# One core, attention with one shared key head beside a Mish MLP: a new order of the products of the first stage

## The chip, the cores and the metric

The kernel runs on one core of one Trainium2 chip. The metric is the device time of one execution in microseconds; three executions of the kernel before took 1537.57 to 1537.7 us, the median is 1537.6.

## What is computed

```python
x = A_x                                    # [1, 2048, 512]
xn = layernorm(x)                          # over the last axis, eps 1e-5, no weights
q = (xn @ wq)                              # 32 heads of 16
k, v = xn @ wk, xn @ wv                    # one head of 16 for all
p = softmax(q k^T / 4)                     # 2048 x 2048 for each head
attention = concat(p v) @ wo               # 512 -> 512
h = xn @ w1 + b1                           # 512 -> 1792
mlp = (h * tanh(softplus(h))) @ w2         # Mish, 1792 -> 512
out = x + attention + mlp
```

All is fp32 outside. Inside, a product of two fp32 tensors is made of three passes over rounded parts: each tensor is stored as an upper part (the value rounded to the narrower format of the TensorE pass) and a lower part (what the rounding left), and the terms upper·upper, upper·lower and lower·upper are summed in one PSUM bank (`TERMS`).

## The kernel before

**Two stages.** The first stage (lines 829 to 1044) loads and normalises the tokens, transposes them, multiplies them by the query and key/value weights, starts two tiles of the MLP, and takes the 32 first pairs of scores, from which the row maxima for the first head group come. The second stage goes through a written plan (`PLAN`, one token per piece of work) with all other scores, exponentials, products with V and MLP tiles. It stays as it was; its first TensorE instruction is a pair of scores at L555.

**Tokens and tiles.** The 2048 tokens are four chunks of 512, called 0 to 3. A chunk has four query tiles of 128 rows (q*c*_*mt*) and one key/value tile (kv*c*). A tile of product is 12 matmuls of 128 x 512 (four slices of the depth, three terms) into one PSUM bank. The key/value tiles of chunks 0 and 1, the first query tile and the two first MLP tiles `hidden(0)` and `hidden(1)` are multiplied in this way, in full height, one after another (L796).

**Products by halves.** From then on, two tiles (a word of two letters: piece k and l are the key/value tiles of chunks 2 and 3, the other letters the next query tiles in order) are multiplied side by side: one step is two matmuls of 64 of the 128 rows (L781), one in each half of the array, one for each tile, each into its own bank. A word has 24 steps: 12 in the first order, then 12 with the halves of the two tiles exchanged. Since the exchanged half adds to a bank that the other half of the array wrote, TensorE drains (L957) before the second order, unless two pairs of scores since then show that the first order is done. `HALVES` lists phases: a word stands for six steps, a digit for half of the transposes of that chunk, the star for one query tile in full height, into bank 7. The pairs of banks for the words are (4, 5) and (6, 7), given out in turn (`places`).

**Pairs of scores.** A pair (`first_pair`, L555) is two matmuls side by side, of 128 queries by 512 keys each, and one reduction on DVE (L572) over both banks; two pairs of banks alternate. The 32 pairs go by key chunk: pairs 0 to 7 read keys 0, pairs 8 to 15 keys 1, and so on; pair 24 is the first to read keys 3. Between two pairs the recorder takes steps by a credit of `PACE` (11, from pair 20 on 9; a step of two matmuls costs 2), so a pair falls into a phase wherever the credit ends.

**What hangs on a product.** When a key/value tile is done, ACT copies it out of its bank (L475) and rounds it into KS (L477), and POOL writes the lower part of the keys, in two steps (L433, `KS<-kvs,KS`). When a query tile is done, ACT copies it out (L507) and rounds it (L513), POOL writes its lower part (L433, `q<-q`), and SP stores it. A transposed chunk gets its lower part on POOL too (L433, `X<-pt,X`). The MLP tiles 0 and 1 go through Mish, a chain of ACT steps (L738 to L753), one short DVE step (L742) and five products (L747, L759 to L763) on POOL; the last four of them are on DVE if all first scores are done when they are recorded.

**What sets the order.** All of this is recorded by one program in the order in which it stands on each engine. Lower parts and Mish are not recorded at once but put off (`later`) by so many pairs, and recorded when due or when their reader is (`flush`); each engine's queue keeps that order and does not pass a waiting instruction.

Of the kernel before, what the change touches and what calls it, by code (L numbers as in the profile page):

```python
# [20 lines left out]
NT = CT // P  # L21
DT = D // P
FT = F // P
KT = S // P
KC = S // CT
# [8 lines left out]
U_MAX = 16384.0  # L34
WARM = 44
QBUFS = 6
PACE = 11, 9
HALVES = "qr 2 qr 2 qr qr tk tk uv tk tk uv 3 uv 3 uv wl wl wl wl xy xy ab ab ab ab xy xy cd cd ef ef cd cd ef ef *"

TERMS = ((0, 0), (0, 1), (1, 0))  # L40

# [139 lines left out]
def attention_and_mlp(ctx: ExitStack, tc: tile.TileContext, x, wq, wk, wv, wo, w1, b1, w2, out):  # L181
    nc = tc.nc
    E = mybir.EngineType
    PE, SP = nc.tensor, nc.sync
# [16 lines left out]
    def bank(tag, name, bufs):  # L201
        return BANK[{"o": 6, "misc": 7}[tag]]

    def misc(name):
        return bank("misc", name, 1)
# [11 lines left out]
    def product_bank():  # L217
        return BANK[given.pop(0)]
# [8 lines left out]
    def later(delay, stage, tag, step=None):  # L227

        queue.append((now[0] + delay if step is None else step, stage, tag))
# [218 lines left out]
    def project(w, c, hi_first=False):  # L448
        order = [(d, i, j) for d in range(DT) for i, j in TERMS]
        if hi_first:  # L450
            order.sort(key=lambda term: term[2])
        return [(w(i, d), X[c][:, j, d]) for d, i, j in order]

    def keys_values(c, every=3):
# [41 lines left out]
    def queries(c, mt):  # L496
        if mt not in WQ:
            WQ[mt] = query_block(mt)
        wb = WQ[mt].rearrange("p a (t f) -> p a t f", t=DT)
        yield 3 * DT, (("wq", mt),)  # L500
        flush(("wq", mt))
        turn[0] += 1
        p = product_bank() if halving[0] else bank("o", f"q{c}_{mt}", 1) if turn[0] % 2 else misc(f"q{c}_{mt}")
        yield p, project(lambda i, d: wb[:, i, d], c, c == mt == 0)
        q = first.tile([P, 2, CT], F32R, tag="q", name=f"q{c}_{mt}", bufs=QBUFS)
        qf = q.bitcast(F32)
        ACT.activation(qf[:, 1], p, AF.Copy)  # L507
        yield
        last = c * DT + mt >= NC * DT - 3
        if last:  # L510
            POOL.tensor_copy(q[:, 0], qf[:, 1])
        else:
            ACT.activation(q[:, 0], qf[:, 1], AF.Copy)  # L513

        def rest():
            below(DVE if scored[0] and not last else POOL, q[:, 1], qf[:, 1], q[:, 0])
            d = scratch.tile([2, P, CT], F32, tag="q", name=f"q{c}_{mt}_dram", bufs=NC * DT)
            for g in range(2):
                u = c * UPC + 2 * mt + g
                if u:  # L520
                    if g == 0 or u == 1:
                        SP.dma_start(out=d.rearrange("k p n -> p k n"), in_=qf)
                    LOADS[u] = lambda u=u, g=g: load(u, g)
                    if u < QTS:
                        later(0, LOADS[u], ("q", u))
                    continue
                QS[u] = QT[u % QTS]
                for a in range(2):
                    r = (2 * g + a) * 2 * DH
                    for k, part in enumerate((0, 1, 0)):  # L530
                        to = a * 64 + k * DH
                        SP.dma_start(out=QS[u][to : to + DH].bitcast(F32), in_=qf[r : r + 2 * DH, part])

            def load(u, g):
                QS[u] = QT[u % QTS]
                for a in range(2):
                    r = (2 * g + a) * 2 * DH
                    for to, n in ((0, 2), (2 * DH, 1)):
                        SP.dma_start(
                            out=QS[u][a * 64 + to : a * 64 + to + n * DH].bitcast(F32),  # L540
                            in_=d[:n, r : r + 2 * DH].rearrange("k (d pair) n -> k d (pair n)", pair=2),
                        )

        later(1, rest, ("q", c, mt))
        yield
# [180 lines left out]
    def hidden(f):  # L726

        yield 3 * DT, (("w1", f),)
        flush(("w1", f))
        p = misc(f"h0_{f}") if f else bank("o", f"h0_{f}", 1)  # L730
        wb = WB[f].rearrange("p a (t f) -> p a t f", t=DT)
        yield p, project(lambda i, d: wb[:, i, d], 0)
        h, n = TH[f], TN[f]
        u, z, r = (first.tile([P, CT], F32, tag=t, name=f"{t}{f}", bufs=1) for t in ("fu", "fz", "fr"))
        ACT.activation(h, p, AF.Identity, bias=b1s[:, f : f + 1])

        def exponential():
            ACT.activation(u, h, AF.Exp)  # L738
            later(1, square, ("u", f))

        def square():
            DVE.tensor_scalar_min(u, u, U_MAX)  # L742
            later(1, product, ("u", f))

        def product():
            ACT.activation(n, u, AF.Copy, bias=2.0)
            POOL.tensor_tensor(out=n, in0=n, in1=u, op=ALU.mult)  # L747
            later(2, quotient, ("u", f))

        def quotient():  # L750
            ACT.activation(z, n, AF.Ln, bias=2.0)
            ACT.activation(r, z, AF.Exp, scale=-1.0)
            mish(h, n, z, r, lambda out, x: ACT.activation(out, x, AF.Copy, scale=-2.0, bias=2.0), DVE if scored[0] else POOL)  # L753

        later(max(1, 8 + 4 * f - 100 - now[0]), exponential, ("u", f))

    def mish(h, n, z, r, affine, engine=POOL):

# [69 lines left out]
    with tc.tile_pool(name="first", bufs=1) as first:  # L828
# [55 lines left out]

        flush(("wq", 0))
        first_transposes()
        split_block()
        first_keys = keys_values(0, 1)
        for _ in range(4):
# [9 lines left out]
        run(first_keys)  # L899
        while first_queries.product():  # L900
            pass
        turned = banks[:, 1, :FT]
        PE.transpose(turned, b1_rows, ident[:FT, :FT])
        ACT.activation(b1s, turned, AF.Copy)
        flush(("q", 0, 0))
        root(1, DVE)
# [21 lines left out]
        def phases():  # L928
            opened, turning = {}, {}
            for word in HALVES.split():  # L930
                if word.isdigit():
                    if word not in turning:
                        turning[word] = transposes_by_halves(int(word))
                    for cost in turning[word]:
                        if not cost:
                            break
                        yield cost
                    continue
                if word == "*":
                    piece = ready.pop(0)  # L940
                    given[:] = [7]
                    while piece.product():
                        done[0] += 1
                        yield 2
                    done[0] += 1
                    continue
                if word not in opened:
                    b = places.pop(0)
                    given[:] = b, b + 1
                    both = [Piece(keys_values_by_halves(2 + (k == "l"))) if k in "kl" else ready.pop(0) for k in word]  # L950
                    for piece in both:
                        piece.begin()
                    opened[word] = b, both, [(order, k) for order in range(2) for k in range(3 * DT)]
                b, both, todo = opened[word]
                for order, k in todo[: 3 * DT // 2]:
                    if order and not k and known[0] < both[-1]:
                        PE.drain()  # L957
                        known[0] = emitted[0]
                    last = [both[lane ^ order].half(k, lane, order) for lane in range(2)]
                    if last[1]:  # L960
                        both[1].end()
                        both[0].end()
                    emitted[0] += 1
                    done[0] += 1
                    if k + 1 == 3 * DT:
                        both.append(emitted[0])
                    yield 2
                del todo[: 3 * DT // 2]
                if not todo:
                    places.append(b)  # L970
                    del opened[word]
                    if not (opened or scores_left[0] or ready):
                        return
# [10 lines left out]
            while n > 0 and ready:  # L984
                n -= fill_slot(n)

        scores_left, credit, steps = [len(range(KC * NT * 2))], 0, phases()
        order = [(kc, qt, pair) for kc in range(KC - 1) for qt in range(NT) for pair in range(2)]
        order += [(KC - 1, qt, pair) for pair in range(2) for qt in range(NT)]
        for i, (kc, qt, pair) in enumerate(order):  # L990
# [4 lines left out]
            if i == 7:  # L995
                root(3, POOL)
                normalise(3, POOL)
            credit += PACE[i >= 20] + (6 if i in (1, 2) else 0)
            while credit > 0:
                credit -= next(steps, credit)  # L1000
            if i == 1:
                rooted(3)
            run_due(2)
            if i == 22:
                for a in range(2):
                    r = slice(a * 64 + 48, a * 64 + 50)
                    SP.dma_start(out=KS[r].bitcast(F32), in_=ones[:, None].to_broadcast([2, KT, P]))
            if i in (7, 9, 15):
                flush(("v", (7, 9, 15).index(i)))
            if 8 <= i < 16 or 20 <= i < 24:  # L1010
                c = (1, 2, 3, 3)[(i - 8) // 4]
                flush(("lo", c))
# [261 lines left out]
```

## Time and profile before

| | |
|---|---|
| median of three executions | 1537.6 us |
| profiled execution, its own time | 1537.76 us |
| its span | 1536.0 us |
| instructions on TensorE, busy | 11767, 1528.4 us |
| first pair of scores starts | 28.95 us |
| first TensorE instruction of the planned stage | 90.84 us |
| mean granted TensorE clock | 1.000 |

In the timeline rows a line starts with the time from the start of the span and the duration, then the engine, the line of the kernel, the operation, the tile written and the tiles read, their shapes and the number of instructions that are put together in the row; a bracket gives how long the engine had stood idle and who released it. PE is TensorE, DVE VectorE, ACT ScalarE, POOL GpSimd. Two matmuls that go side by side in the two halves of the array start within some nanoseconds of each other, and each has a record of its own. In a table of windows, "x" counts matmuls that lie in the window.

### The profile page before, as it was taken

To read this page: it belongs to the slowest core of one execution; us is meant where nothing else is said; L and a number is where in the kernel's file an instruction comes from. 1 tells how busy PE (TensorE), PEld (TensorE's weight loads), DVE (VectorE), ACT (ScalarE), POOL (GpSimd) and SP (SyncE) were. 2 spreads that over 40 slices of the span, in tenths; PEclk is the share of its full clock that TensorE was granted. 3 is DMA by queue.
4 is the path that set the end of the run, shared out by engine and by line. 5 is a ranking of instruction groups with operands and counts; after the bars stand their busy time and mean duration, and the time that the engine had idled before them with its cause. 6 is when DMAs were issued, how large, how long until landed. Compare 5 with 4: busy or idle time off the path is not lost.

```text
span 1536.0 us, 30659 instructions
## 1 busy us (share of the span) xinstructions
PE 1528.4 (100%) x11767; PEld 852.0 (55%) x11767; DVE 1353.4 (88%) x2166; ACT 1298.2 (85%) x2301; POOL 887.4 (58%) x838
## 2 busy tenths in 40 slices
PE   9999999999999999999999999999999999999998
PEld 7865555555555555545555555555555545555555
DVE  7899899898998898999989999989988998999842
ACT  6478888988989888887888888888888888888896
POOL 6769675776656546644655575454255844554641
PEclk9999999999999999999999999999999999999999
DMA  5755122243122231142413231033222133032220
GB/s 188 291 195 191 42 81 87 101 151 113 38 65 80 94 101 40 54 135 95 123 41 127 94 108 51 31 115 117 71 88 91 56 92 94 32 101 95 70 92 34
DMA packets 65479, 148.37 MB, mean 97 GB/s; under 512 B 10886, under 2 KB 20180, under 8 KB 64948
## 3 DMA queue, kind: packets, MB, share of 16 engines
q1 hardware_dynamic: 65332, 146.41, 29.2%
q8 instruction: 93, 1.52, 0.4%
q14 instruction: 54, 0.44, 0.1%
HBM read 98.51 MB, written 47.45 MB: 95 GB/s over the span
## 4 chain that ended last, share of the span: by engine, by line
PE 98%; POOL 1%; DVE 0%; ACT 0%; DMA 0%; issue 0%; SPq 0%; POOLq 0%
PE banks L637 33%; PE banks L1084 24%; PE banks L633 19%; PE banks L555 18%; PE banks L781 3%; PE banks L796 1%; PE banks L718 1%; PE banks L458 0%; POOL X L433 0%; DMA pt<-in_A_x_dram 0%; DVE ysb L708 0%; PE banks L397 0%; PE banks L419 0%; POOL KS L433 0%; POOL wq L433 0%
## 5 line engine op out<-in xcount | busy, mean ns | idle before, releaser
L567 DVE TENSOR_REDUCE nm<-banks 128x1 f32<-128x512 f32 x1770 | 1117.2, 684 | 107.5 <-PE banks L555 62.2
L1160 ACT ACTIVATE pt<-banks 128x512 f32<-128x512 f32 x1618 | 871.4, 603 | 130.8 <-PE banks L633 70.6
L555 PE MATMUL banks<-KS,QS 48*128 48x512 f32 x2048 | 688.0, 420 | 0.0
L633 PE MATMUL banks<-QS,KS 64*128 64x512 f32 x2048 | 686.9, 417 | 0.0
L637 PE MATMUL banks<-pt,V 128*32 128x512 f32 x4096 | 534.5, 603 | 0.0
L633 PEld LDWEIGHTS banks<-QS,KS 64*128 64x128 f32 x2048 | 333.1, 184 | 220.4 <-DVE nm L567 81.1
L555 PEld LDWEIGHTS banks<-KS,QS 48*128 48x128 f32 x2048 | 329.4, 184 | 196.5 <-DVE nm L567 94.1
L1084 PE MATMUL banks<-ring,act 64*128 64x512 f32 x1344 | 333.4, 397 | 0.2
L1084 PE MATMUL banks<-X,wblk 64*128 64x512 f32 x1296 | 330.2, 395 | 0.3
L1152 ACT ACTIVATE pt<-banks 128x1024 f32<-128x1024 f32 x215 | 219.5, 1025 | 47.7 <-PE banks L633 27.6
L1084 PEld LDWEIGHTS banks<-X,wblk 64*128 64x128 f32 x1296 | 214.0, 185 | 27.9 <-issue 10.7
L1084 PEld LDWEIGHTS banks<-ring,act 64*128 64x128 f32 x1344 | 213.1, 185 | 28.7 <-issue 12.0
L637 PEld LDWEIGHTS banks<-pt,V 128*32 128x32 f32 x4096 | 86.5, 108 | 181.7 <-issue 172.1
L759 POOL TENSOR_TENSOR tn<-tn,tr 128x512 f32<-128x512 f32 x54 | 69.4, 1285 | 192.8 <-ACT tr L1170 192.8
L1165 POOL TENSOR_SCALAR tu<-tu 128x512 f32<-128x512 f32 x54 | 80.3, 1487 | 157.5 <-ACT tu L1164 157.5
L581 DVE TENSOR_REDUCE nm<-banks 128x2 f32<-128x1024 f32 x107 | 130.1, 1219 | 10.6 <-PE banks L555 6.5
L1098 POOL TENSOR_TENSOR ysb<-ysb,ty 128x512 f32<-128x512 f32 x64 | 82.1, 1286 | 86.9 <-ACT ty L1097 86.9
L251 POOL TENSOR_TENSOR act<-th,act 128x512 fp32r<-128x512 f32 x56 | 72.1, 1287 | 32.8 <-ACT act L250 24.0
L761 POOL TENSOR_TENSOR tz<-tz,tn 128x512 f32<-128x512 f32 x54 | 69.5, 1288 | 4.5
L1167 POOL TENSOR_TENSOR tn<-tn,tu 128x512 f32<-128x512 f32 x54 | 69.5, 1288 | 4.5
L763 POOL TENSOR_TENSOR th<-th,tz 128x512 f32<-128x512 f32 x54 | 69.6, 1288 | 4.2
L762 POOL TENSOR_TENSOR th<-th,tn 128x512 f32<-128x512 f32 x55 | 70.9, 1289 | 0.0
(140 smaller groups left out, 1042.0 us busy)
## 6 DMA issues: line engine op xcount, KB each, us to landing
wblk<-w_dram SPq DMA_DIRECT2D x42, 512.0 KB
ring<-w_dram SPq DMA_DIRECT2D x42, 512.0 KB
q_dram<-q SPq DMA_DIRECT2D x16, 512.0 KB
QS<-q_dram SPq DMA_DIRECT2D x62, 128.0 KB
o_dram<-ov SPq DMA_DIRECT2D x31, 256.0 KB
raw_w<-in_B_w_dram SPq DMA_DIRECT2D x28, 256.0 KB
w_dram<-wblk SPq DMA_DIRECT2D x14, 512.0 KB
w_dram<-ring SPq DMA_DIRECT2D x14, 512.0 KB
```

The source lines that it names most:

```text
L251: POOL.tensor_tensor(out=lo, in0=src, in1=hi.bitcast(F32), op=ALU.subtract)
L555: PE.matmul(tile, QS[u][rows, pair, qt * P : (qt + 1) * P], KS[rows, kc * CT : (kc + 1) * CT], start=True, stop=True,)
L567: DVE.tensor_reduce(out=m[:, a : a + 1], in_=tile, axis=AX.X, op=ALU.max)
L581: DVE.tensor_reduce(out=m, in_=tiles, axis=AX.X, op=ALU.max)
L633: PE.matmul(bank, KS[rows, kt * P : (kt + 1) * P], QS[u][rows, pair], start=True, stop=True)
L637: PE.matmul(BANK[7][h * 32 : (h + 1) * 32], V[:, kt], PT.pop((u * KT + kt) * HG + h), start=kt == 0, stop=kt == KT - 1,)
L762: engine.tensor_tensor(out=h, in0=h, in1=n, op=ALU.mult)
L1084: PE.matmul(self.p, w[rows], x[rows], start=self.first, stop=not any(self.todo))
L1098: POOL.tensor_tensor(out=YS[t], in0=YS[t], in1=ty, op=ALU.add)
L1152: ACT.activation(slots[slot // 2], banks[:, bank : bank + 2], AF.Exp, scale=SCALE)
L1160: ACT.activation(PT[n], BANK[bank], AF.Exp, scale=SCALE)
L1165: POOL.tensor_scalar_min(tu, tu, U_MAX)
```

## The change

`HALVES` is written anew, as phases with a point wherever a pair of scores is to stand; `PACE` and its credit go. Up to the two words wl and xy a phase has six steps as before, with a pair between phases; from the second half of wl on, a phase has four steps (`:4`), so three pairs stand between the three phases of half a product. Seven words are multiplied by halves instead of eight, and the last three query tiles (`*6 *4 *7`, the digit is the bank) in full height instead of one. The first query tile goes to bank 7's pool (`misc`) where it went to bank 6, the transpose of b1 is put ahead of the first products, the terms of the first products stand in another order (`hi_first`), Mish of the MLP tiles starts two pairs' time sooner, and the V steps are recorded at pairs 7, 12 and 17.

```diff
-PACE = 11, 9
-HALVES = "qr 2 qr 2 qr qr tk tk uv tk tk uv 3 uv 3 uv wl wl wl wl xy xy ab ab ab ab xy xy cd cd ef ef cd cd ef ef *"
+HALVES = (
+    ". qr . qr 2 . qr 2 . qr . tk . tk . uv . uv . tk . tk . uv . 3 . uv . 3 "
+    ". xy . xy . wl . wl . xy . xy . wl:4 . wl:4 . wl:4 . ab:4 . ab:4 . ab:4 . cd:4 . cd:4 . cd:4 . ab:4 . ab:4 . ab:4 "
+    "cd cd *6 *4 *7"
+)
...
-            order.sort(key=lambda term: term[2])
+            order.sort(key=lambda term: (term[2], term[1]))
...
-        p = product_bank() if halving[0] else bank("o", f"q{c}_{mt}", 1) if turn[0] % 2 else misc(f"q{c}_{mt}")
+        p = product_bank() if halving[0] else misc(f"q{c}_{mt}")
...
-        later(max(1, 8 + 4 * f - 100 - now[0]), exponential, ("u", f))
+        later(max(1, 6 + 4 * f - 100 - now[0]), exponential, ("u", f))
...
+        turned = banks[:, 1, :FT]
+        PE.transpose(turned, b1_rows, ident[:FT, :FT])
         split_block()
...
-        turned = banks[:, 1, :FT]
-        PE.transpose(turned, b1_rows, ident[:FT, :FT])
...
             for word in HALVES.split():
+                word, _, n = word.partition(":")
+                n = int(n or 3 * DT // 2)
...
-                if word == "*":
+                if word == ".":
+                    yield 0
+                    continue
+                if word[0] == "*":
                     piece = ready.pop(0)
-                    given[:] = [7]
+                    given[:] = [int(word[1])]
...
-                for order, k in todo[: 3 * DT // 2]:
+                for order, k in todo[:n]:
...
-            credit += PACE[i >= 20] + (6 if i in (1, 2) else 0)
-            while credit > 0:
-                credit -= next(steps, credit)
+            while scores_left[0] and next(steps):
+                pass
...
-            if i in (7, 9, 15):
-                flush(("v", (7, 9, 15).index(i)))
+            if i in (7, 12, 17):
+                flush(("v", (7, 12, 17).index(i)))
```

Three places show how the instructions move (line numbers of the kernel after are 3 larger up to about L766 and 8 larger at the end).

POOL, around the lower parts of the keys of chunk 3 (`KS<-kvs_871` before), before the change; tn, fz and th with 76, 360 and 73 belong to Mish of MLP tile 0:

```order
L433 TENSOR_TENSOR q_1_786<-q_1_786 128x512
L433 TENSOR_TENSOR q_0_789<-q_0_789 128x512
L433 TENSOR_TENSOR KS<-kvs_871,KS 16x512 x2
L433 TENSOR_TENSOR q_2_874<-q_2_874 128x512
L747 TENSOR_TENSOR tn_76<-tn_76,fu_359 128x512
L759 TENSOR_TENSOR tn_76<-tn_76,fr_361 128x512
L761 TENSOR_TENSOR fz_360<-fz_360,tn_76 128x512
L762 TENSOR_TENSOR th_73<-th_73,tn_76 128x512
L763 TENSOR_TENSOR th_73<-th_73,fz_360 128x512
```

The same place after the change (`KS<-kvs_952`):

```order
L436 TENSOR_TENSOR q_1_749<-q_1_749 128x512
L436 TENSOR_TENSOR q_0_752<-q_0_752 128x512
L750 TENSOR_TENSOR tn_76<-tn_76,fu_359 128x512
L436 TENSOR_TENSOR q_3_894<-q_3_894 128x512
L436 TENSOR_TENSOR q_2_897<-q_2_897 128x512
L762 TENSOR_TENSOR tn_76<-tn_76,fr_361 128x512
L764 TENSOR_TENSOR fz_360<-fz_360,tn_76 128x512
L765 TENSOR_TENSOR th_73<-th_73,tn_76 128x512
L766 TENSOR_TENSOR th_73<-th_73,fz_360 128x512
L436 TENSOR_TENSOR KS<-kvs_952,KS 16x512 x2
L436 TENSOR_TENSOR q_0_955<-q_0_955 128x512
```

Before, the two key steps stood ahead of Mish and behind the lower parts of two queries; now they stand behind the four last steps of Mish, behind the lower parts of the two queries of xy (q_3_894, q_2_897).

TensorE, around pair 24, the first that reads keys 3, with what each waits for, before; the products are those of the word ab (wq_120, wq_122):

```order
L781 MATMUL banks<-X_470,wq_120 128x512
L781 MATMUL banks<-X_470,wq_122 128x512
L781 MATMUL banks<-X_470,wq_120 128x512
L781 MATMUL banks<-X_470,wq_122 128x512
L555 MATMUL banks<-KS,QS_88 128x512 [waits DVE_49,Pool_49]
L555 MATMUL banks<-KS,QS_88 128x512 [waits Pool_49]
L781 MATMUL banks<-X_470,wq_120 128x512
L781 MATMUL banks<-X_470,wq_122 128x512
```

After, from pair 23 on; the last step of wl stands directly ahead of these rows:

```order
L558 MATMUL banks<-KS,QS_88 128x512 [waits DVE_49]
L558 MATMUL banks<-KS,QS_88 128x512
L784 MATMUL banks<-X_482,wq_120 128x512 [waits Activation_49]
L784 MATMUL banks<-X_482,wq_122 128x512
L784 MATMUL banks<-X_482,wq_120 128x512
L784 MATMUL banks<-X_482,wq_122 128x512
L784 MATMUL banks<-X_482,wq_120 128x512
L784 MATMUL banks<-X_482,wq_122 128x512
L784 MATMUL banks<-X_482,wq_120 128x512
L784 MATMUL banks<-X_482,wq_122 128x512
L558 MATMUL banks<-KS,QS_88 128x512 [waits DVE_49,Pool_49]
L558 MATMUL banks<-KS,QS_88 128x512 [waits Pool_49]
```

The pair waits for POOL in both. In the new order the last step of wl stands one pair and one phase of four steps ahead of it; in the old one wl's last step (`X_705,wkv` with `X_363,wq_122`, at the place below) stands four whole pairs with the phases of xy and ab between them ahead:

```order
L555 MATMUL banks<-KS,QS_88 128x512 [waits DVE_49]
L555 MATMUL banks<-KS,QS_88 128x512
L781 MATMUL banks<-X_705,wkv 128x512
L781 MATMUL banks<-X_363,wq_122 128x512
L781 MATMUL banks<-X_363,wq_128 128x512 [waits Activation_49]
L781 MATMUL banks<-X_470,wq_103 128x512
```

TensorE at the end of the first stage, before; wq_128 in full height is the star, and the L555 below it the planned stage's first:

```order
L781 MATMUL banks<-X_705,wq_122 128x512
L781 MATMUL banks<-X_705,wq_120 128x512
L796 MATMUL banks<-X_705,wq_128 128x512 [waits Activation_49]
L796 MATMUL banks<-X_705,wq_128 128x512 x11
L555 MATMUL banks<-KS,QS_89 128x512 [waits DMAHW3_49,DMAHW2_49,Activation_49]
L633 MATMUL banks<-QS_88,KS 128x512 [waits DMAHW5_49,DMAHW3_49,DVE_49]
```

After:

```order
L784 MATMUL banks<-X_714,wq_103 128x512
L784 MATMUL banks<-X_482,wq_128 128x512
L799 MATMUL banks<-X_714,wq_120 128x512 [waits Activation_49]
L799 MATMUL banks<-X_714,wq_120 128x512 x11
L799 MATMUL banks<-X_714,wq_122 128x512 x12
L799 MATMUL banks<-X_714,wq_128 128x512 x12
L558 MATMUL banks<-KS,QS_89 128x512 [waits DMAHW3_49,DMAHW2_49,Activation_49]
L636 MATMUL banks<-QS_88,KS 128x512 [waits DMAHW4_49,DMAHW3_49,DVE_49]
```

One tile in full height has become three; both times the first of them waits for ACT, and the others wait for nothing.

More of the change, by code (lines that the diff above doesn't have):

```diff
@@ L967, in phases @@
                     yield 2
-                del todo[: 3 * DT // 2]
+                del todo[:n]
                 if not todo:
@@ L985, in fill_slots @@
                 n -= fill_slot(n)
-        scores_left, credit, steps = [len(range(KC * NT * 2))], 0, phases()
+        scores_left, steps = [KC * NT * 2], phases()
+        next(steps)
         order = [(kc, qt, pair) for kc in range(KC - 1) for qt in range(NT) for pair in range(2)]
```

## The prediction, made before the changed kernel was run

> **What bounds the kernel now.** First the page: busy shares, and the chain of work that ended last.
>
> ```profile
> PE 1528.4 (100%) x11767; PEld 852.0 (55%) x11767; DVE 1353.4 (88%) x2166; ACT 1298.2 (85%) x2301; POOL 887.4 (58%) x838
> ...
> PE 98%; POOL 1%; DVE 0%; ACT 0%; DMA 0%; issue 0%; SPq 0%; POOLq 0%
> ```
>
> TensorE works all the time and is itself the chain: a microsecond in which it stands anywhere is a microsecond on the end. So I read the timeline of PE over the first stage, where all edits lie, up to its last query tile and the first pair of scores of the planned stage.
>
> ```profile
> 28.95 0.50 PE L555 MATMUL banks<-KS,QS 48*128 48x512 f32 x2
> ...
> 64.20 0.41 PE L555 MATMUL banks<-KS,QS 48*128 48x512 f32 x2
> ...
> 65.36 0.41 PE L555 MATMUL banks<-KS,QS 48*128 48x512 f32 x2
> ...
> 67.92 0.41 PE L555 MATMUL banks<-KS,QS 48*128 48x512 f32 x2
> ...
> 69.67 0.40 PE L555 MATMUL banks<-KS,QS 48*128 48x512 f32 x2
> ...
> 87.85 3.06 PE L796 MATMUL banks<-X,wq 128*128 128x512 f32 x12
> 90.84 0.50 PE L555 MATMUL banks<-KS,QS 48*128 48x512 f32 x1
> ```
>
> Pairs of scores start at 28.95; the planned stage starts at 90.84 and its instructions are the same after the change, so the change is worth what it moves 90.84. From 64.20 to 65.36 stand one pair and four steps: five slots in 1.16 us, **0.233 us a slot** (a slot is one pair or one step, each two matmuls side by side). Between 28.95 and 90.84 both kernels have the same 236 slots. So the change can only move waits, drains and the clock.
>
> **The change part by part.** *The start.* The eviction of the first query tile holds the bank into which the first MLP tile is multiplied.
>
> ```profile
> 16.57 1.08 PE L796 MATMUL banks<-X,wq 128*128 128x512 f32 x4
> 17.58 0.23 PE L903 MATMUL banks<-ident,b_rows 14*128 14x14 f32 x1
> 18.57 3.02 PE L796 MATMUL banks<-X,wblk 128*128 128x512 f32 x12 [0.76 <-ACT q L507]
> ```
>
> With the query in the other bank and the b1 transpose earlier, the 0.76 goes, and with it about 0.1 of restart and 0.1 in the new order of the first terms: **−1.0** (−0.7 to −1.2).
>
> *Drains.* Six slots from 67.92 to 69.67 should take 6 × 0.233 = 1.40 and took 1.75: the drain ahead of the second order of a product costs 0.35. The old program has six of these at L957 and the new one has one: 5 × 0.35 = **−1.75**.
>
> *Old waits.* A pause between two steps ends at 57.46:
>
> ```profile
> 57.02 0.39 PE L781 MATMUL banks<-X,wq 64*128 64x512 f32 x1
> 57.46 0.49 PE L781 MATMUL banks<-X,wkv 64*128 64x512 f32 x1
> ```
>
> 0.44 instead of a slot's 0.233, and a like one for the tokens before it: **−0.3**.
>
> *New small waits.* The products come sooner after their tokens. The lower parts of chunk 2 end on POOL at 34.95 + 4.92 = 39.87; TensorE asks for them at about 39.6, by slots counted from the new first pair at 27.9 (an estimate):
>
> ```profile
> 34.95 4.92 POOL L433 TENSOR_TENSOR X<-pt,X 128x1024 fp32r<-128x1024 f32 x2
> ```
>
> I put 0.4 there, 0.35 where xy takes the banks that uv has just left, 0.15 for chunk 3: **+0.9** (0 to 1.3; nothing below, as a wait gives no time).
>
> *The keys of chunk 3* (the piece called l, in wl). Pair 24 is the first to read them, and waits for POOL's two lower-part steps. Before, wl was multiplied out at 61.64, eight microseconds ahead of pair 24 at 69.67:
>
> ```profile
> 61.64 0.39 PE L781 MATMUL banks<-X,wkv 64*128 64x512 f32 x1
> ...
> 62.12 0.60 ACT L475 ACTIVATE kvs<-banks 128x512 f32<-128x512 f32 x1 [4.70 <-issue]
> ...
> 63.09 0.63 ACT L477 ACTIVATE KS<-kvs 128x512 fp32r<-128x512 f32 x1
> ...
> 63.86 2.66 POOL L433 TENSOR_TENSOR KS<-kvs,KS 16x512 fp32r<-16x512 f32 x2 [3.97 <-ACT KS L477]
> ```
>
> Done at 66.52, they were 3.15 us early. Now wl ends one pair and four steps ahead of pair 24: from its last half, 6 slots = 1.4 us, while the rows above need 66.52 − 61.64 = 4.9. That alone is a wait of 3.5. POOL's order makes it longer: two lower parts of xy's queries and four steps of Mish now stand ahead of the two key steps, which stood ahead of Mish before. The durations:
>
> ```profile
> 72.44 1.09 ACT L507 ACTIVATE q<-banks 128x512 f32<-128x512 f32 x2 [0.79 <-PE banks L781]
> 73.42 1.16 ACT L513 ACTIVATE q<-q 128x512 fp32r<-128x512 f32 x2
> ```
>
> ```profile
> 71.13 1.29 POOL L759 TENSOR_TENSOR tn<-tn,fr 128x512 f32<-128x512 f32 x1 [2.00 <-ACT fr L752]
> 72.50 1.50 POOL L761 TENSOR_TENSOR fz<-fz,tn 128x512 f32<-128x512 f32 x1
> 73.95 1.29 POOL L762 TENSOR_TENSOR th<-th,tn 128x512 f32<-128x512 f32 x1
> 75.32 1.30 POOL L763 TENSOR_TENSOR th<-th,fz 128x512 f32<-128x512 f32 x1
> 76.58 2.54 POOL L433 TENSOR_TENSOR q<-q 128x512 fp32r<-128x512 f32 x2
> ```
>
> From the start of xy's last half: 0.41 for it, 1.61 until the first query is rounded (72.44 to about 74.05), 0.1 over to POOL, 2.54 for two queries, 5.49 for Mish (71.13 to 76.62), 0.08, 2.66 for the keys, 0.08 back: 13.0. ACT's part of that Mish (about 1.9, behind the two evictions) ends 0.3 before POOL wants it. TensorE gets to pair 24 in 21 slots = 4.9. The wait is 13.0 − 4.9 = **+8.1** (7.0 to 8.4). Everything on TensorE is behind it, as the pair stands in order. Mish itself has no reader before the planned stage.
>
> *The clock.* In that wait the first matmul of pair 24 is released by the first key step, 1.33 before the second, so TensorE does nothing for some 6.5 us. What an idle array costs is seen at both ends of the trace:
>
> ```profile
> 1.35 7.53 PE L851 MATMUL banks<-ident 128*128 128x128 f32 x44 [1.35 <-POOL ident masks.py:199]
> ```
>
> ```profile
> 1524.46 7.64 PE L718 MATMUL banks<-ring,ohl 128*128 128x512 f32 x30
> ```
>
> ```profile
> core 0: us, PE busy (x), PEclk, DMA share, GB/s
> 4.50:6.50 2.00, 2.00 (x11) 1.00 1.03 309
> 6.60:8.60 2.00, 2.00 (x20) 1.00 1.00 320
> 1532.00:1534.00 2.00, 0.10 (x1) 1.00 0.95 350
> 1534.00:1536.00 2.00, 0.00 (x0) 0.93 0.29 108
> ```
>
> At the start the transposes run at half rate (11 in 2 us, then 20) from 1.35 to about 6.5: 5.2 us. (PEclk has no record there and shows 1.00; the counts tell.) At the end the last matmul ends at 1532.10, and the mean of 0.93 in the last window puts the fall to half (0.07 × 2 / 0.5 = 0.28 us of it) 3.6 us later. An idle of 6.5 is longer than 3.6, so I expect half rate, and for as long as at the start: 5.1 × 0.45 = **+2.3** (0 to 3.1). The Trainium skill, "TensorE: Matmul & The Clock Gate", Part 1 (The HAM clock gate), says that a free-running window of about 3.4 us without work halves the clock and about 3.4 us of sustained work restores it. The fall at 3.6 agrees; by its figure the return would be quicker than the start shows, and the estimate from the page would be 3.4 × 0.5 = 1.7 instead of 2.3.
>
> *Three full tiles.* The first of them goes to bank 6, which the second piece of cd has just left, and waits for its eviction:
>
> ```profile
> 87.94 1.09 ACT L507 ACTIVATE q<-banks 128x512 f32<-128x512 f32 x2 [0.67 <-PE banks L781]
> ```
>
> From the start of the last half: 0.41, then both evictions, 1.09, and 0.06 over: the next product starts 1.56 later instead of after a slot and a change (0.32): **+1.25** (1.1 to 1.4). The other two tiles have banks long free. Their 24 matmuls take the place of as many slots, at the same rate: twelve in the 2.99 us from 87.85 to 90.84 are 0.233 each but for 0.2 of changes.
>
> *Nothing.* Pairs every five slots ask DVE for one reduction in 1.16 us:
>
> ```profile
> 63.25 1.23 DVE L572 TENSOR_REDUCE nm<-banks 128x2 f32<-128x1024 f32 x1 [0.17 <-PE banks L555]
> 64.65 2.38 DVE L572 TENSOR_REDUCE nm<-banks 128x2 f32<-128x1024 f32 x2 [0.17 <-PE banks L555]
> ```
>
> One takes 1.23 and two together 2.38, so they follow each other at 1.15: DVE just keeps pace; 0, at most +0.4. Mish of the second MLP tile goes from DVE to POOL, which stands idle once the keys are done; the V steps stay ahead of their first use. The late queries' evictions and loads are covered by the planned stage.
>
> **The sum:** −1.0 − 1.75 − 0.3 + 0.9 + 8.1 + 2.3 + 1.25 = +9.5. The profiled execution took 1537.76 us (span 1536.0), the median is 1537.6: 1547.26 profiled, **1547.1** as a median. A measurement here tells some 0.2% = 3.1 us from no change.
>
> **The rivals.**
>
> A, the forecast: full wait and half clock: 1547.1, on its own bounds 1545 to 1549.5. Chance 0.68.
>
> B, the full wait, but the clock holds: the first key step breaks the idle time, or the windows fall well. 9.5 − 2.3 = +7.2: 1544.8. The end of the trace speaks against it (3.6 is enough). 0.16.
>
> C, the key steps are late by their own chain only: wait 3.5, of which 2.2 idle, no fall of the clock. 9.5 − 8.1 − 2.3 + 3.5 = +2.6: 1540.2. It needs POOL's six foreign steps (2.54 + 5.49 = 8.0 us) to be done when the rounding of the keys is, 2.2 us (61.64 to 63.86) after wl; no row shows a POOL step of this shape under 1.27. 0.05.
>
> D, the other side: pair 24 doesn't stand at all, as the old kernel has a POOL wait there too and passed it with 3.15 to spare. It decides at the point where the key steps end within 4.9 us of xy's last half; then the sum is 9.5 − 8.1 − 2.3 = −0.9: 1536.7, no measurable change; with the full tile's and small waits away as well, −3.1 or faster. Against it: wl's own chain needs 4.9 us and has 1.4. 0.08, of it 0.02 faster by over 0.2%.
>
> E, worse: DVE falls behind at the five-slot pace, or the half clock lasts longer: over 1549.5. 0.03.
>
> **How the numbers follow.** The likeliest case gives 1547.1. The range is A and B with the bounds of the wait, the clock and the tile: 1543.0 (B with the wait at 7.0 and the start and tile at their best) to 1549.5; C, D and E, 0.16, lie outside. Slower by over 0.2%: A, B, E = 0.87. Same: C and the rest of D = 0.11. Faster: 0.02.
>
> **What would show it.** First pair at about 27.9, one drain left, xy's last half near 62.7. Then a hole in PE from about 67.7 to 75.5 ahead of a pair, released by POOL's key step, with POOL's key row at 72.9 or so, straight behind Mish; half as many matmuls in 2 us as elsewhere for some 5 us behind it. A pause of 1.5 ahead of the first full query tile; the planned stage's first pair near 100. If that hole is missing or under 4 us, the forecast is wrong; if the hole is there and the steps behind it run at a slot of 0.233, B is right.

## The result, and the profile after

| | before | after |
|---|---|---|
| median, us | 1537.65 (4 runs, 1537.57 to 1538.37) | 1546.45 (4 runs, 1545.95 to 1547.4) |
| profiled execution, its span | 1537.76, 1536.0 | 1547.4, 1545.6 |
| first pair of scores | 28.95 | 28.72 |
| first instruction of the planned stage | 90.84 | 100.59 |
| from there to the end of the span | 1445.2 | 1445.0 |
| mean granted clock | 1.000 | 0.997 |

The changed kernel takes 1.0057 times as long (95% interval 1.0039 to 1.0074), 8.8 us by the medians. The last but one row of the table says where: the planned stage is as long as before, and all of it is lost ahead of it, 9.75 us in the profiled execution (the slowest of the four). One execution of mish_later, below, took 3619.12 us at full clock; it is in no ratio, and without it that kernel's median of 1543.68 would be 1543.52.

The page's busy line of the changed kernel, to be read beside the old one:

```profile
PE 1530.8 (99%) x11743; PEld 852.8 (55%) x11743; DVE 1350.8 (87%) x2164; ACT 1297.2 (84%) x2301; POOL 888.6 (57%) x840
```

TensorE has 24 instructions fewer and is busy 2.4 us longer; the rest of the loss is time in which it stands. The list of waits names it: what TensorE waited for between 28 and 101 us (line waiting, engine and tile waited for; total, times, longest):

```profile
PE banks L558 <- POOL KS L436: 6.5, 2, 6.0
PE banks L799 <- ACT q L510: 1.0, 1, 1.0
```

TensorE's timeline around the first of them, pair 24:

```profile
67.30 1.32 PE L784 MATMUL banks<-X,wq 64*128 64x512 f32 x8
74.59 0.79 PE L558 MATMUL banks<-KS,QS 48*128 48x512 f32 x1 [5.97 <-POOL KS L436]
75.92 0.79 PE L558 MATMUL banks<-KS,QS 48*128 48x512 f32 x1 [0.54 <-POOL KS L436]
...
77.80 1.05 PE L558 MATMUL banks<-KS,QS 48*128 48x512 f32 x2
...
79.93 1.05 PE L558 MATMUL banks<-KS,QS 48*128 48x512 f32 x2
...
82.03 0.62 PE L558 MATMUL banks<-KS,QS 48*128 48x512 f32 x2
```

The four steps ahead of pair 24 start at 67.30, so its two matmuls were due at 68.23 and 68.46 (here the two halves of the array run one slot, 0.233 us, apart, and not within nanoseconds); they start at 74.59 and 75.92, each released by one of POOL's key steps. Behind the hole the pairs stand 2.1 us apart instead of 1.16, up to 82.03. POOL's timeline over the same time shows what it did instead of the keys:

```profile
65.45 2.55 POOL L436 TENSOR_TENSOR q<-q 128x512 fp32r<-128x512 f32 x2 [1.79 <-ACT q L516]
67.96 1.28 POOL L762 TENSOR_TENSOR tn<-tn,fr 128x512 f32<-128x512 f32 x1
69.32 1.32 POOL L764 TENSOR_TENSOR fz<-fz,tn 128x512 f32<-128x512 f32 x1
70.61 1.25 POOL L765 TENSOR_TENSOR th<-th,tn 128x512 f32<-128x512 f32 x1
71.94 1.26 POOL L766 TENSOR_TENSOR th<-th,fz 128x512 f32<-128x512 f32 x1
73.28 2.59 POOL L436 TENSOR_TENSOR KS<-kvs,KS 16x512 fp32r<-16x512 f32 x2
```

It never stands from 65.45 to 75.87: two lower parts of xy's queries, four steps of Mish, then the keys. The windows of TensorE (busy, matmuls, granted clock, share of DMA, GB/s) show the clock:

```profile
70.00:72.00 2.00, 0.00 (x0) 0.94 1.05 396
72.00:74.00 2.00, 0.00 (x0) 0.50 1.00 312
...
80.00:82.00 2.00, 2.00 (x12) 0.50 0.75 213
82.00:84.00 2.00, 2.00 (x20) 1.00 0.01 3
```

The mean of 0.94 puts the fall at about 71.8 (0.06 x 2 / 0.5 = 0.24 us of half clock in that window), 3.1 us after TensorE's last matmul; half clock lasts until about 82, 7.4 us into the work that follows.

The last row is the first full query tile, and the planned stage behind the three of them:

```profile
91.99 8.67 PE L799 MATMUL banks<-X,wq 128*128 128x512 f32 x36 [0.96 <-ACT q L510]
100.59 0.50 PE L558 MATMUL banks<-KS,QS 48*128 48x512 f32 x1
```

### The profile page after: what moved, and what is told of

Same layout as the page of the kernel before. It is cut to its first block, busy times and chain, and to the rows that moved or that the text cites. A ratio compares the mean times of both kernels' runs of the same rounds, so it can differ in the third digit from the quotient of the medians.

```text
span 1545.6 us, 30611 instructions
## 1 busy us (share of the span) xinstructions
PE 1530.8 (99%) x11743; PEld 852.8 (55%) x11743; DVE 1350.8 (87%) x2164; ACT 1297.2 (84%) x2301; POOL 888.6 (57%) x840
## 4 chain that ended last, share of the span: by engine, by line
PE 97%; POOL 1%; DMA 1%; issue 0%; DVE 0%; ACT 0%; SPq 0%; POOLq 0%
PE banks L640 33%; PE banks L1092 23%; PE banks L636 19%; PE banks L558 18%; PE banks L784 2%; PE banks L799 1%; PE banks L721 1%; POOL q L436 0%; DMA x_dram<-X 0%; PE banks L461 0%; DMA b_rows<-in_B_b_dram 0%; DMA pt<-in_A_x_dram 0%; POOL KS L436 0%; DVE ysb L711 0%; PE banks L400 0%
## 5 line engine op out<-in xcount | busy, mean ns | idle before, releaser
L558 PEld LDWEIGHTS banks<-KS,QS 48*128 48x128 f32 x2048 | 334.4, 185 | 204.7 <-DVE nm L570 94.1
L766 POOL TENSOR_TENSOR th<-th,tz 128x512 f32<-128x512 f32 x54 | 69.5, 1287 | 4.2
```

What stands on the lines that cost most here:

```text
L558: PE.matmul(tile, QS[u][rows, pair, qt * P : (qt + 1) * P], KS[rows, kc * CT : (kc + 1) * CT], start=True, stop=True,)
```

## The experiments

The theory: pair 24 waits for POOL's key steps, because wl ends late and Mish stands ahead of them; the idle time halves the clock; the other terms are small. The rivals: the loss lies in the new places of the pairs, in the full tiles, or would turn up at another wait as soon as the hole is filled. Each kernel was timed in five rounds beside the kernel before on the same chip, one of three (its median there 1537.75 to 1537.98); the ratios are to that.

**mish_later**

```diff
-        later(max(1, 6 + 4 * f - 100 - now[0]), exponential, ("u", f))
+        later(max(1, 8 + 4 * f - 100 - now[0]), exponential, ("u", f))
```

> One edit to the changed kernel: Mish of the MLP tiles starts at 8 + 4f again, so its four last steps stand behind POOL's two key steps. Theory (the hole ahead of pair 24 is POOL's queue): the key steps then start when the lower parts of xy's queries and one Mish step are done, 67.96 + 1.3 = 69.3, and end at 71.9 instead of 75.87: 4.0 us less. TensorE is then idle for some 2 us and not 6, so the clock should hold, and the 2.5 us of half clock go too: 1546.45 - 4.0 - 2.5 = about 1540.0; if the clock falls all the same, 1542.5. Rival (the pairs' new places and the three full tiles are what costs, the hole would be filled by another wait): within 1 us of 1546.45.

Measured: 1543.68, ratio 1.0035 (1.0022 to 1.0048). That is 1.2 over the higher of the two numbers; the hole shrank as expected, but the clock did fall. TensorE's timeline at pair 24, and its windows:

```profile
71.59 0.50 PE L558 MATMUL banks<-KS,QS 48*128 48x512 f32 x1 [2.29 <-POOL KS L436]
72.92 0.50 PE L558 MATMUL banks<-KS,QS 48*128 48x512 f32 x1 [0.83 <-POOL KS L436]
```

```profile
72.00:74.00 2.00, 1.17 (x9) 0.92 1.05 374
74.00:76.00 2.00, 2.00 (x12) 0.50 1.01 340
76.00:78.00 2.00, 2.00 (x16) 0.73 0.75 294
```

The hole shrinks from 7.2 to 3.6 us, by 3.6 where 4.0 was expected. But the clock falls at about 73.7, when TensorE has been at work again for 0.8 us: an unbroken idle of more than 3.1 us isn't needed. And Mish done later brings waits of its own, in the same trace 0.6 us at a pair (DVE then has a step of Mish, 1.26 us long, between two reductions) and 0.8 in the planned stage. The start of this profile, 0.9 later than that of the changed kernel, belongs to b1 (below). So Mish's place is worth half the hole; what it gains is partly given back.

**busy_wait**

```diff
         e = pair_bank(f"s0_{qt}_{kc}_{pair}")
+        if (kc, qt, pair) == (KC - 1, 0, 0):
+            for i in range(52):
+                PE.transpose(e[:, 0, i % NT * P : (i % NT + 1) * P], ident, ident)
```

> One edit to the changed kernel: 52 transposes of the identity into pair 24's own bank stand ahead of pair 24 on TensorE; the pair overwrites what they wrote. They take some 5.2 us of the 6 us in which TensorE stands. Theory (idle time lowers the clock): the hole keeps its length, pair 24 starts at the same time, and the steps behind it run at 0.233 us a slot: 2.5 us less, 1544.0. Rival (the slow steps behind the hole come from something else that the wait leaves, such as ACT or DVE catching up): 1546.4, or more by what the transposes add.

Measured: 1544.82, ratio 1.0046 (1.0034 to 1.0058). TensorE's timeline:

```profile
68.08 5.89 PE L576 MATMUL banks<-ident 128*128 128x128 f32 x52
74.20 0.50 PE L558 MATMUL banks<-KS,QS 48*128 48x512 f32 x1 [0.22 <-POOL KS L436]
75.53 0.50 PE L558 MATMUL banks<-KS,QS 48*128 48x512 f32 x1 [0.84 <-POOL KS L436]
...
76.56 0.62 PE L558 MATMUL banks<-KS,QS 48*128 48x512 f32 x2
77.73 0.62 PE L558 MATMUL banks<-KS,QS 48*128 48x512 f32 x2
```

Useless work in the hole makes the kernel faster. Pair 24 still waits for POOL, but the pairs behind it follow at 1.17 us, and the planned stage starts 69.2 us after the first pair of scores (28.24 to 97.45) instead of 71.87: 2.7 us less in the profile, 1.6 by the medians. Its mean granted clock is 1.000 in four executions and 0.999 in the fifth (the one of 1547.26 us, as slow as the changed kernel); the changed kernel has 0.997 in all four. The half clock is due to the idle array.

**keys_sooner**

```diff
-    ". xy . xy . wl . wl . xy . xy . wl:4 . wl:4 . wl:4 . ab:4 ...
+    ". xy . xy . wl . wl . wl . wl . xy:4 . xy:4 . xy:4 . ab:4 ...
```

> One edit to the changed kernel: in the list of phases wl's four phases of six stand together and xy's second half gets the three phases of four behind them, so wl ends 14 slots sooner and POOL's key steps stand ahead of Mish. Theory: wl ends where xy ended (63.4), the key steps end 4.9 us later at 68.3, when pair 24 is due (68.5 and 0.35 for a drain that comes back): no hole and no half clock, 1546.45 - 7.4 - 2.5 + 0.35 = about 1537.0. Rival (the hole only moves: to the rows of chunk 3 that wl needs sooner, or to xy's evictions): between 1541 and 1546.

Measured: 1537.7, ratio 0.9998 (0.9990 to 1.0007). POOL's and TensorE's timelines:

```profile
65.76 2.66 POOL L436 TENSOR_TENSOR KS<-kvs,KS 16x512 fp32r<-16x512 f32 x2 [2.46 <-ACT KS L480]
```

```profile
68.46 0.50 PE L558 MATMUL banks<-KS,QS 48*128 48x512 f32 x2
...
81.88 8.66 PE L799 MATMUL banks<-X,wq 128*128 128x512 f32 x36 [0.78 <-ACT q L510]
90.47 0.50 PE L558 MATMUL banks<-KS,QS 48*128 48x512 f32 x1
```

One exchange of words takes back the whole loss: the key steps end at 68.42 and pair 24 starts at 68.46, with no hole and no fall of the clock. The rival is out. What is left of the change is worth nothing: from the first pair to the planned stage it takes 62.1 us (28.34 to 90.47), the old kernel 61.9.

**b1_behind**

```diff
         first_transposes()
-        turned = banks[:, 1, :FT]
-        PE.transpose(turned, b1_rows, ident[:FT, :FT])
         split_block()
...
+        turned = banks[:, 1, :FT]
+        PE.transpose(turned, b1_rows, ident[:FT, :FT])
         ACT.activation(b1s, turned, AF.Copy)
```

> One edit to the changed kernel: the transpose of b1 is put back behind the first products. In the trace of the changed kernel it waits 1.47 us for b1's load, with the first products queued behind it on TensorE; first products start at 12.80 there and at 11.46 before. Theory (that wait ate the gain of the start): the first MLP tile starts some 0.75 sooner, 1545.7. Rival (the products wait for the rows of X anyway, so the place of the transpose costs nothing): 1546.4.

Measured: 1546.58, ratio 1.0055 (1.0043 to 1.0067): no gain in the median, so the times don't bear out the theory. In its trace the first pair stands at 28.27; where the transpose waits for b1's load, the first pair follows how long that takes. The row of the changed kernel, and of mish_later, which has the same start:

```profile
12.64 0.23 PE L891 MATMUL banks<-ident,b_rows 14*128 14x14 f32 x1 [1.47 <-DMA b_rows<-in_B_b_dram]
```

```profile
13.54 0.23 PE L891 MATMUL banks<-ident,b_rows 14*128 14x14 f32 x1 [2.56 <-DMA b_rows<-in_B_b_dram]
...
29.63 0.50 PE L558 MATMUL banks<-KS,QS 48*128 48x512 f32 x2
```

Waits of 1.27 and 1.06 (keys_sooner, busy_wait) give a first pair at 28.34 and 28.24, 1.47 gives 28.72, 2.56 gives 29.63. Up to some 1.2 us the wait is hidden, since the products would wait for the rows of X; beyond that it counts in full, and it differs from one profiled execution to the next: in bank4_first, which has the start of the changed kernel, it is 0.77 and the first pair stands at 28.16. It can cost more than its length, too: in keys_bank4's trace a wait of 1.61 is followed by half clock from 12.22 to 15.63, and the first pair stands at 29.95.

**keys_bank4** and **keys_bank4_b1**

```diff
-    "cd cd *6 *4 *7"
+    "cd cd *4 *6 *7"
```

> keys_sooner with a second edit: the three full tiles go to banks 4, 6, 7 instead of 6, 4, 7. Theory (the first full tile waits for the eviction of cd from bank 6): bank 4 has been free for 14 slots, the pause of 0.94 + 0.11 ahead of the first full tile shrinks to a change of 0.1, and 6 is free when its tile comes: 1537.7 - 0.95 = about 1536.75. Rival (the planned stage waits for something else that is late then, the maxima or the loads of the next queries): 1537.5 or more.

> keys_bank4 with the transpose of b1 put back behind the first products. Theory: the wait for b1's load at the start was 1.06 to 2.56 us in four profiles, of which only what is beyond about 1.1 reaches the first pair of scores, so the median gains 0 to 0.4 and the spread of the times shrinks: about 1536.5, the fastest of all kernels here. Rival (the start is not moved at all): the same as keys_bank4.

Measured: 1541.82, ratio 1.0028 (1.0016 to 1.0040), and 1541.21, ratio 1.0022 (1.0013 to 1.0031). About four microseconds slower than keys_sooner, where one was to be gained; the 0.6 between the two lies within their spreads. In keys_sooner wl gives its banks back before xy, so cd comes to lie in banks 4 and 5; the edit takes the bank that was left last. TensorE's row in keys_bank4:

```profile
85.93 10.20 PE L799 MATMUL banks<-X,wq 128*128 128x512 f32 x36 [3.29 <-ACT q L510]
```

The wait is 3.4 us longer than a change of product, and the 36 matmuls take 10.20 instead of 8.66, at half clock for part of them:

```profile
88.00:90.00 2.00, 2.00 (x6) 0.50 1.02 373
```

My reading of which bank is free was wrong for that order; that the first full tile waits for its bank's eviction is confirmed the hard way.

**bank4_first**, the same edit on the changed kernel itself, where cd lies in 6 and 7:

> One edit to the changed kernel: the three full tiles go to banks 4, 6, 7 instead of 6, 4, 7. In the changed kernel cd lies in banks 6 and 7 and ab in 4 and 5 (in keys_sooner it was the other way round, and bank 4 was the wrong one to take first). Theory: bank 4 was evicted two microseconds before it is asked for, so the pause of 1.1 ahead of the first full tile goes, 6 is free when its tile comes: 1546.5 - 1.0 = about 1545.5, all else as in the changed kernel. Rival (the pause returns ahead of the second full tile or at the start of the planned stage): 1546.5.

Measured: 1545.62, ratio 1.0050 (1.0037 to 1.0062), 0.8 less than the changed kernel; the intervals overlap, so the time alone doesn't show it. TensorE's rows:

```profile
86.11 3.90 PE L784 MATMUL banks<-X,wq 64*128 64x512 f32 x31
89.94 8.66 PE L799 MATMUL banks<-X,wq 128*128 128x512 f32 x36
98.53 0.50 PE L558 MATMUL banks<-KS,QS 48*128 48x512 f32 x1
```

The pause ahead of the first full tile is gone (0.08 over a slot instead of 1.11), and no other takes its place.

**keys_all_drains**

```diff
-                    if order and not k and known[0] < both[-1]:
+                    if order and not k:
```

> keys_sooner with a second edit: TensorE drains before the second order of each of the seven words, five drains more than it has. Theory (a drain costs the 0.35 that was read off one pair of rows): 1537.7 + 5 x 0.35 = about 1539.4. Rival (the drain hides in a wait that is there anyway, or the next matmul would have to wait for its bank): 1537.7 to 1538.2.

Measured: 1538.39, ratio 1.0004 (0.9995 to 1.0012), 0.7 over keys_sooner, too little to be told from it by time. In the trace each drain costs the 0.35 to 0.4, but two waits that keys_sooner has are gone: ahead of the first full tile 0.2 instead of 1.05, and 0.26 at a pair. Five drains make 1.75, less 1.1: 0.65. Here a drain cost its price only where nothing behind it waited anyway.

**old_mish_sooner**

```diff
-        later(max(1, 8 + 4 * f - 100 - now[0]), exponential, ("u", f))
+        later(max(1, 6 + 4 * f - 100 - now[0]), exponential, ("u", f))
```

> The kernel before with one edit, Mish of the MLP tiles at 6 + 4f. POOL's key steps stay ahead of Mish there, since wl ends four pairs ahead of pair 24. Theory (Mish sooner costs only by standing ahead of the key steps): no change, 1537.65 within 0.4. Rival (Mish sooner costs by itself, by POOL's time or by taking bandwidth from DVE): 1539 or more.

Measured: 1541.19, ratio 1.0022 (1.0014 to 1.0031): 3.2 us slower, and my theory of this edit was wrong. What TensorE waited for from 28 to 101 us:

```profile
PE banks L555 <- DVE nm L572: 1.2, 2, 0.7
PE banks L633 <- DMA QS<-m_dram: 0.9, 1, 0.9
```

Its DVE step, with the same step in the kernel before:

```profile
55.22 2.23 DVE L742 TENSOR_SCALAR fu<-fu 128x512 f32<-128x512 f32 x1 [0.93 <-ACT fu L738]
57.37 1.21 DVE L572 TENSOR_REDUCE nm<-banks 128x2 f32<-128x1024 f32 x1
```

```profile
61.48 0.43 DVE L742 TENSOR_SCALAR fu<-fu 128x512 f32<-128x512 f32 x1
```

Moved to 55.22 it takes 2.23 us instead of 0.43; POOL has two long steps there, the lower parts of chunk 3 (the last section shows them). The reductions queue behind it and TensorE waits 1.2 us at two pairs, and 0.9 more for the maxima at the planned stage: 2.1 of the 2.9 by which this trace is longer than that of the kernel before. In the changed kernel the same step lies at 57.10, beside POOL's idle 1.57, and takes 0.43: sooner Mish costs nothing there but its place in POOL's queue.

**keys_sooner_mish_later**, **keys_mish_b1** and **old_bank7**

```diff
-        p = product_bank() if halving[0] else bank("o", f"q{c}_{mt}", 1) if turn[0] % 2 else misc(f"q{c}_{mt}")
+        p = product_bank() if halving[0] else misc(f"q{c}_{mt}")
...
-            order.sort(key=lambda term: term[2])
+            order.sort(key=lambda term: (term[2], term[1]))
```

(The diff is old_bank7's; the other two join edits shown above.)

> keys_sooner with Mish at 8 + 4f again. In keys_sooner the last wait is 0.94 ahead of the first full tile: ACT evicts ab only behind three steps of Mish for the second MLP tile (78.89 to 80.85). Theory (Mish sooner is now only in the way): those steps come later, the pause goes, 1537.7 - 1.0 = about 1536.7. Rival (Mish later puts four products on DVE when the planned stage starts, as at 99.14 in mish_later, where TensorE waited 0.8 for them): 1537.5 or more.

> keys_sooner_mish_later with the transpose of b1 put back behind the first products. Theory: the wait for b1's load reached the first pair in two of seven profiles so far (28.7 to 29.95 instead of 28.25), so the median gains 0.3 and the highest times come down: about 1536.4. Rival (the products of the start wait for the rows of X anyway): the same as keys_sooner_mish_later.

> The kernel before with two edits of the change alone: the first query tile goes to bank 7, and the first terms stand in the new order; the transpose of b1 stays behind. Theory (the start's gain is real and is eaten by the wait for b1): the wait of 0.76 ahead of the first MLP tile goes, the first pair of scores starts at about 28.2 instead of 28.95: 1537.7 - 0.7 = about 1537.0. Rival (what follows waits for the rows of chunk 1 or for key chunk 0 instead): 1537.7.

Measured: 1538.1, ratio 1.0004 (0.9995 to 1.0013); 1537.91, ratio 1.0003 (0.9994 to 1.0011); 1537.22, ratio 0.9998 (0.9989 to 1.0007). None can be told from the kernel before. In keys_sooner_mish_later the pause ahead of the full tile goes, as expected, and what it saved turns up at two other places:

```profile
PE banks L636 <- DVE nm L570: 0.8, 1, 0.8
PE banks L558 <- DVE nm L575: 0.5, 1, 0.5
```

In old_bank7 the first pair stands at 27.86 instead of 28.95, and the planned stage at 89.92 instead of 90.84, so the start's gain is there in the trace, some 0.9 us. By the medians it is 0.55, within what the interval leaves open. No version here beats both kernels by more than the measurement can tell.

## Why the prediction was right, step by step

Forecast 1547.1, measured 1546.45. The terms, from gaps between neighbouring starts on TensorE that exceed a slot, in the two profiled executions:

| term | forecast | measured |
|---|---|---|
| start | −1.0 | −0.2 |
| five drains | −1.75 | −1.7 |
| old waits gone | −0.3 | −0.45 |
| new small waits | +0.9 | +0.75 |
| pair 24 | +8.1 | +7.2 |
| half clock | +2.3 | +2.8 |
| first full tile | +1.25 | +1.0 |
| sum | +9.5 | +9.4, of 9.75 |

The 0.35 that is left over is in smaller gaps. That the sum came so near is in part luck: the start missed by +0.8 and the hole by −0.9, and the two cancel. The cause, pair 24 behind POOL's key steps, is not luck.

*The hole* was right in place and cause, and 0.9 too long. The chain from xy's last half (62.17 and five slots, 63.34) to pair 24's second matmul (75.92) took 12.6 instead of 13.0, most of the difference in Mish (5.24, from 67.96 to 73.20, instead of 5.49); TensorE came 0.2 later than my 21 slots; and pair 24's first matmul does a slot's work within the wait. keys_sooner shows the cause of the hole by intervention, and busy_wait that of the half clock; mish_later shows that Mish is some half of the hole and wl's late end the rest.

*The clock* fell as in case A. My step "an idle of 6.5 is longer than 3.6, so I expect half rate" gave the right answer by too simple a rule: in mish_later it fell after a hole of 3.6 that a matmul broke. Kernels with the same hole paid differently. These are the windows in which half clock ended in b1_behind and in bank4_first:

```profile
78.00:80.00 2.00, 2.00 (x17) 0.83 1.01 349
```

```profile
80.00:82.00 2.00, 2.00 (x19) 0.91 0.51 149
```

0.83 and 0.91 put the return at 78.7 and 80.4, 4.5 and 6.3 us after pair 24's first matmul (74.17, 74.03); in the changed kernel it was 7.4. In slots lost behind the hole that is 1.5, 2.4 and 2.8 us. So "for as long as at the start" is not what set the size: the same hole cost 1.5 in one execution and 2.8 in another, and that the forecast of 2.3 lay near the 2.8 is luck.

The clock's records in the three traces show what set it. Half clock lasts from 71.84 to 78.67 in b1_behind, from 70.14 to 80.38 in bank4_first and from 71.74 to 81.98 in the changed kernel: two, three and three times 3.41 us. Within these steps of 3.41 us TensorE was busy for 0.79 and then 3.17 us in b1_behind; for 0, 2.40 and 3.41 in bank4_first; for 0.56, 2.88 and 3.41 in the changed kernel. In each, full clock follows the first step that is nearly all work, and the work began somewhere within an earlier step. The Trainium skill, "TensorE: Matmul & The Clock Gate", Part 1 (The HAM clock gate), calls its window of about 3.4 us free-running. The steps of 3.41 agree; a window that doesn't start with the work is why the return came 4.5 to 7.4 us after the first matmul here. The estimate of 1.7 from that figure lies, as the 2.3 from rows does, within the 1.5 to 2.8 measured.

*The start* is the term that failed: "the 0.76 goes" is true (the first MLP tile follows the products at once in the new trace), but I costed the transpose of b1 at nothing in its new place. It waits for its load, with all first products queued behind it. old_bank7, which leaves the transpose where it was, has the forecast gain (27.86 against 28.95 in the profiles). The −0.2 is that of one execution: with bank4_first's wait of 0.77 the same start gives 28.16, −0.8. No medians tell the two places of the transpose apart (b1_behind), so this cause is read from traces and not shown by time.

*The small waits* came to the forecast's sum by other places: at chunk 2's lower parts (forecast 0.4) 0.25, and where xy takes the banks of uv, 0.43.

*The rivals.* B fell by the clock rows, C and D by the hole. D's argument against itself, that wl's own chain needs 4.9 us and has 1.4, holds in mish_later: without Mish's four steps ahead, 3.6 us of hole remain. That this is C's number of 3.5 is partly chance: one other step of Mish (68.92, 1.27 long) still stands ahead of the keys there, and POOL starts them at 70.27, half a microsecond after ACT has rounded them (69.14, 0.63 long), so wl's own chain accounts for about 3.1. C's assumption that the clock then holds was wrong.

## What to carry to other kernels

When an order is rewritten to pack one engine, follow for each reader the whole chain of its last producer through the other engines' queues: here a product's end moved from 34 slots ahead of its reader (8.0 us) to 6, two small steps of another engine fell behind eight microseconds of work nobody was waiting for, and a gain of drains turned into a loss five times its size. A hole on TensorE can cost more than its length, as the clock falls with it (1.5 to 2.8 us more for the same hole of 7.2 here, by chance of the moment), and work without a purpose in the hole can be cheaper than none. Moving an instruction ahead of a load's landing puts everything queued behind it at the mercy of that load.

## What was not expected of the hardware

The granted clock changes only in whole steps of one length. In all fourteen traces every stretch from one change of the clock to the next is a whole number of steps of 3.41 us: 19 from 6.89 to 71.74 in the changed kernel, 448 from 6.54 to 1535.71 in the kernel before. The first change lies between 4.66 and 7.14, differently from trace to trace, and so all steps lie differently against the work.

The clock fell also without a long unbroken idle. In keys_mish_b1 the longest wait near the fall was about one microsecond; the row, and two steps of the clock around it:

```profile
92.25 0.49 PE L636 MATMUL banks<-QS,KS 64*128 64x512 f32 x1 [0.99 <-DVE nm L570]
```

```profile
90.52:93.93 3.41, 2.31 (x15) 1.00 0.97 358
93.93:97.34 3.41, 3.41 (x15) 0.50 0.88 289
```

The profile of keys_sooner_mish_later has nearly the same waits and kept 1.00 throughout. There the steps cut the waits in two:

```profile
88.56:91.97 3.41, 2.97 (x16) 1.00 1.03 380
91.97:95.39 3.42, 2.99 (x19) 1.00 0.96 353
```

So a fall can hang on where the steps lie, which no line of the kernel sets: the times of keys_mish_b1 spread from 1537.3 to 1540.7. In the first 110 us of all traces there are eight falls; in seven of them TensorE was busy for 1.80 us or less of the 3.41 ahead of the fall, here for 2.31. A step with 1.95 busy (10.30 to 13.72 in the changed kernel) was not followed by one. And in keys_mish_b1 the first step of full work, the second row above, did not bring full clock back; the next did, at 100.75. What the gate weighs within a step isn't settled by these runs.

A DVE step of one operand, 0.43 us by itself, took 2.23 in old_mish_sooner. It began half a microsecond into the second of these two POOL steps and ended 0.3 after it:

```profile
52.40 4.76 POOL L433 TENSOR_TENSOR X<-pt,X 128x1024 fp32r<-128x1024 f32 x2
```

The other traces make this a rule. The step (`fu<-fu`, one for each of the first two MLP tiles) stands twice in each of the fourteen. The 14 that began with POOL idle took 0.42 to 0.43 us, and so did one that began as POOL ended. The 13 that began within a POOL step took 0.49 to 2.23, and every one of them ended 0.28 to 0.29 after that POOL step; the 1.26 us in mish_later is one (78.48 to 79.74, POOL's step from 78.15 to 79.45). So it is POOL's step that it waits out. The Trainium skill, "SBUF — State Buffer", Who interferes with whom, says that such a DVE step can need a port pair that a POOL instruction holds to its end, and then stands for all of it. These times agree; that it is a port pair is the skill's account, which no time here can show.
